# Gate logits of a Sinkhorn mixture of experts: float32 products from the accumulators in place of products on the split forms

## The chip, the cores and the metric

One core of one Trainium2 chip. The metric is the device time of one execution in microseconds, the median of several runs. Half a per cent of it is 10.6 us.

## The reference

Three parts run in a row. A linear attention on features gives x (2304 tokens by 512). A feed-forward with squared relu maps it: `h = relu(x @ w_in)`, `x = (h*h) @ w_out`. Then comes a mixture of 8 experts whose gates are made doubly normalised (a Sinkhorn iteration):

```python
logits = x @ w_gate
logits = logits - logits.max()
P = np.exp(logits)
for _ in range(8):
    P /= P.sum(1, keepdims=True) + 1e-09
    P /= P.sum(0, keepdims=True) + 1e-09
    P *= N / E
for e in range(E):
    out += P[:, e:e + 1] * (np.maximum(x @ w1[e], 0.0) @ w2[e])
```

The change concerns the line `logits = x @ w_gate` (2304x512 by 512x8) and the moment at which the Sinkhorn iteration starts.

## The kernel before

**Number forms.** TensorE (PE) runs almost everything on float32r operands. To keep precision, each operand is split into a high part (a cast on ScalarE, ACT) and a low part (a subtraction on VectorE, DVE); `split_form`, L604 to L606, makes both. A product is then three matmuls: high by high, high by low, low by high.

**First feed-forward.** Four passes of 512 hidden units. In the last pass (L749 to L779, `last`) the tokens are six blocks of 384. A block is four hidden tiles (`layer1`, then `split_square`) and the second layer (`layer2_square`), whose results DVE adds into the accumulators `accT` (L582). Side work is hung into this order by hand: a list `side` of generators, of which `tick()` (L558) advances the first by one step. There are six ticks a block: one after each hidden tile (L764), two inside the second layer (L583).

**Forms of x.** The second feed-forward works on pairs of blocks (768 tokens, three pairs) with seven products in place of eight, so it wants seven forms of x for each pair: four blocks of x and three further sums (t1 to t4 with the names of L627). `forms(q)` (L615) makes them for pairs 0 and 1 as side work in blocks 2 to 5 of the last pass, seven steps each, and writes them to DRAM (`xv`). The forms of pair 2 are made late, inside the second feed-forward, by `last_form` (L708, stores at L733).

**Gate logits.** They are computed from the split forms. `gate_weights` (L546) makes two padded stationary tiles `wg1`, `wg2` from w_gate. In `forms`, after a form that is one of the four in `USES` (L609), `wg1` meets its high part and `wg2` its low part (L645: 40 matmuls of 384 columns over both pairs). Then the 16 rows are turned into token order by four groups of three PE transposes (L657) and land in `lt`. For pair 2 the nested `logits` (L924) does it the other way round in the first layer of step 2: the form is the stationary operand, 16 columns of weights move, into spare columns of a PSUM bank (L935: 60 matmuls).

**Second feed-forward.** 16 passes (two for each expert) by three pairs give 48 steps, `order` (L673), numbered n = 0 to 47. First the first layer of step 0 runs alone (L1057 to L1063). Then, in the loop at L1069, "step n" is the second layer of n beside the first layer of n+1, seven slots each, with two ticks a slot. A slot of a layer is `product` (L862): 12 matmuls of 384 columns. `load_forms` (L695) keeps four forms of x loaded ahead on the SP queue.

**Sinkhorn.** `sinkhorn` (L809) is side work, added after step 1 (L1111), when `logits` has done pair 2. It adds the two halves of `lt` (L810), reduces a maximum, sends it through DRAM on the SP queue (store L813, load L815), waits eight ticks, and does eight rounds of three ticks. A round is nine small DVE instructions (L825 to L830, L837 to L840) around one float32 matmul of 8 columns (L835), which sums over partitions into spare columns of a first-layer bank. At its end four stores write the gates to DRAM (`prT`, L851).

**Use of the gates.** `load_gate` (L854) loads a gate on the SP queue. After step 3, `gate_first` (L1030) is added to the side work: it multiplies the accumulators of pair 0 by the gate of expert 0 (L1038), and so on for pairs 1 and 2. From step 5 on the hidden values of expert 1 and later are gated as they are made (L958).

**Order.** The Tile framework places the instructions of each engine in one fixed order, by the order in which they were traced and by what a planner takes to be ready. `issue_after` puts instructions behind a named one on its engine. Each engine then works in order.

Of the kernel before, what the change touches and what calls it, by code (L numbers as in the profile page):

```python
# [8 lines left out]
F32 = mybir.dt.float32  # L9
# [11 lines left out]
def tile_features_attention__moe__sinkhorn_moe(  # L21
# [19 lines left out]
    P = 128  # L41
# [496 lines left out]

    wg = mb.tile([P, KD, NE], F32, name="wg")
    nc.sync.dma_start(wg, w_gate.rearrange("(k p) e -> p k e", p=P))  # L540
    wg1 = mb.tile([P, KD, P], F32R, name="wg1")
    wg2 = mb.tile([P, KD, P], F32R, name="wg2")
    lt = mb.tile([P, NTT, 2 * NE], F32, name="lt")
    pr = mb.tile([P, NTT, NE], F32, name="pr")

    def gate_weights():  # L546
        z = hp.tile([P, 512], F32, tag="r", bufs=HB["r"], name="z")
        nc.gpsimd.memset(z, 0.0)
        z = z.rearrange("p (k m) -> p k m", k=KD)
        nc.vector.tensor_copy(wg1, z)  # L550
        nc.vector.tensor_copy(wg2, z)
        nc.vector.tensor_copy(wg1[:, :, 0:NE], wg)
        nc.vector.tensor_copy(wg2[:, :, 0:NE], wg)
        nc.vector.tensor_sub(wg1[:, :, NE : 2 * NE], wg, wg1[:, :, 0:NE].bitcast(F32))
# [53 lines left out]

    USES = {"b21": [(0, 1)], "t1": [(1, 0)], "b11": [(0, 0), (1, 0)], "b22": [(1, 1)]}  # L609

# [4 lines left out]
    def forms(q, pool):  # L615
# [8 lines left out]
        pg = [psm.tile([P, 512], F32, tag="sm", name="psg") for _ in range(2)]  # L624
        done = [0, 0]
        of = {}
        for nm in ("b21", "t1", "b11", "b22", "t2", "t4", "t3"):  # L627
# [14 lines left out]
            for blk, k in USES.get(nm, ()):  # L642
                for i in range(KH):
                    for w, part in ((wg1, 0), (wg2, 1)):
                        nc.tensor.matmul(  # L645
                            pg[blk][:, :NB], w[:, KH * k + i], v[:, part, i],
                            start=(done[blk] == 0), stop=(done[blk] == 4 * KH - 1 + 2 * KH * blk),
                        )
                        done[blk] += 1
            yield  # L650
        for blk in range(2):
            gs = pool.tile([2 * NE, NB], F32, tag="gs", name="gs")
            nc.scalar.copy(gs, pg[blk][: 2 * NE, :NB])
            pt = psm.tile([P, 4, 2 * NE], F32, tag="sm", name="pt")
            nt = NB // P
            for i in range(nt):
                nc.tensor.transpose(pt[:, i], gs[:, i * P : (i + 1) * P], ident[: 2 * NE, : 2 * NE])  # L657
            i0 = 2 * NB * q // P + blk * nt
            nc.scalar.copy(lt[:, i0 : i0 + nt], pt[:, :nt])
            yield  # L660
# [88 lines left out]
    for p in range(1, N1):  # L749
# [10 lines left out]
        for bi, (t0, n) in enumerate(blocks):  # L760
# [12 lines left out]
            if bi == 0 and p == 1:  # L773
                gate_weights()
# [376 lines left out]
```

## Time and profile before

| what | us |
|---|---|
| runs | 2109.52, 2110.79, 2118.28 |
| median | 2110.79 |
| the profiled execution | 2115.51 |
| its span, first to last instruction | 2113.7 |

1.8 us of the profiled execution lie outside its span, and it stands 4.7 us above the median. In views of the trace an engine's name stands before the line of the kernel; PE is the matmul itself and PEld the load of its stationary operand, which runs beside the matmul ahead of it. An arrow "a<-b" is output from inputs, and "[5.33 <-DVE hv L606]" says that the engine had been idle for 5.33 us and what ended it.

### The profile page before, as it was taken

Reading aid. Unit: us, or ns where it says so; the run is one execution under the profiler, and the core shown is the slowest. Engines: PE = TensorE matmul, PEld = TensorE weight load, DVE = VectorE, ACT = ScalarE, POOL = GpSimd, SP = SyncE. Lnnn points to the kernel's source line nnn. Section 1 sums busy time; section 2 is a strip of 40 time slices with the busy share of each in tenths; the row PEclk is TensorE's granted clock in tenths of the full one; section 3 lists DMA queues with packets and bytes.
Section 4 is the critical chain, followed back from the end, with each engine's and each line's share of the span. In section 5 each row is a group of like instructions: output and inputs, shape, how many; then the busy total and the mean of one; then the engine's idle time right before and its main releaser. Section 6 shows DMA issues by size and latency. Waiting matters only on the chain.

```text
span 2113.7 us, 31720 instructions
## 1 busy us (share of the span) xinstructions
PE 2066.9 (98%) x12376; PEld 1928.1 (91%) x12376; DVE 1731.3 (82%) x2168; ACT 873.7 (41%) x1505; POOL 765.6 (36%) x426
## 2 busy tenths in 40 slices
PE   8999999999999998899999999999999999999998
PEld 5556679888999998899999999999999999999998
DVE  4888665766567787799989889899898998989986
ACT  6786644222234552433433334333333333333332
POOL 3342300010105442534545435444344444444431
PEclk9999999999999999999999999999999999999999
DMA  4444232100136454767666776666766667676663
GB/s 112 109 106 120 72 115 71 60 29 32 55 148 243 183 195 136 235 226 251 220 226 204 237 246 227 224 211 225 252 221 224 226 222 242 224 227 235 209 203 120
DMA packets 184340, 376.47 MB, mean 178 GB/s; under 512 B 73600, under 2 KB 114560, under 8 KB 184192
## 3 DMA queue, kind: packets, MB, share of 16 engines
q1 hardware_dynamic: 184192, 374.44, 53.6%
q8 instruction: 99, 1.62, 0.3%
q14 instruction: 49, 0.40, 0.1%
HBM read 349.32 MB, written 24.93 MB: 177 GB/s over the span
## 4 chain that ended last, share of the span: by engine, by line
PE 83%; DVE 10%; DMA 4%; ACT 2%; issue 1%; SPq 0%; POOL 0%; DVEq 0%; ACTq 0%; POOLq 0%
PE psb L869 30%; PE psa L869 29%; PE ps L241 6%; PE ps L242 6%; PE ps L243 6%; DVE xl L606 2%; DMA rb<-rden 1%; DVE acc L1008 1%; PE kvp L350 1%; PE psn L406 1%; DVE hv L606 1%; PE zp L357 1%; DVE r L958 1%; DVE w2v L606 1%; PE psd L415 1%
## 5 line engine op out<-in xcount | busy, mean ns | idle before, releaser
L869 PE MATMUL psa<-xl,xh 128*128 128x384 f32 x2400 | 448.4, 336 | 7.2 <-DVE xl L606 4.2
L869 PE MATMUL psb<-xl,xh 128*128 128x384 f32 x2400 | 446.7, 335 | 4.4 <-DVE xl L606 1.7
L869 PEld LDWEIGHTS psa<-xl,xh 128*128 128x128 f32 x2400 | 420.4, 189 | 8.8 <-DVE xl L606 5.0
L869 PEld LDWEIGHTS psb<-xl,xh 128*128 128x128 f32 x2400 | 419.8, 188 | 5.9 <-DVE xl L606 2.3
L897 POOL TENSOR_TENSOR t<-r,r 128x768 f32<-128x768 f32 x96 | 208.7, 2174 | 492.3 <-DVE r L958 453.4
L897 POOL TENSOR_TENSOR t<-r,t 128x768 f32<-128x768 f32 x96 | 232.3, 2419 | 22.8 <-ACT r L962 12.2
L606 DVE TENSOR_TENSOR xl<-t,xl 128x768 fp32r<-128x768 f32 x128 | 187.0, 1463 | 1.4 <-ACT xl L605 1.2
L1008 DVE TENSOR_TENSOR acc<-psb,acc 128x768 f32<-128x768 f32 x163 | 155.0, 951 | 39.7 <-PE psb L869 36.3
L1008 DVE TENSOR_TENSOR acc<-psa,acc 128x768 f32<-128x768 f32 x161 | 153.0, 950 | 37.3 <-PE psa L869 34.0
L869 PE MATMUL psb<-xl,w2v 128*128 128x384 f32 x960 | 180.2, 334 | 0.0
L869 PE MATMUL psa<-xl,w2v 128*128 128x384 f32 x960 | 180.2, 334 | 0.0
L605 ACT CAST xl<-t 128x768 fp32r<-128x768 f32 x128 | 107.3, 838 | 154.8 <-POOL t L897 64.5
L869 PEld LDWEIGHTS psb<-xl,w2v 128*128 128x128 f32 x960 | 167.5, 188 | 0.0
L869 PEld LDWEIGHTS psa<-xl,w2v 128*128 128x128 f32 x960 | 167.4, 188 | 0.0
L605 ACT CAST xl<-r 128x768 fp32r<-128x768 f32 x96 | 80.4, 838 | 160.2 <-PE psa L869 77.2
L606 DVE TENSOR_TENSOR xl<-r,xl 128x768 fp32r<-128x768 f32 x96 | 134.7, 1403 | 7.1 <-ACT xl L605 7.1
L390 POOL PARTITION_ALL_REDUCE eq<-eq x64 | 88.8, 1429 | 141.5 <-ACT eq L389 141.5
L241 PE MATMUL ps<-xh,w0h 128*128 128x288 f32 (+3 forms) x384 | 130.8, 341 | 4.2 <-ACT r L262 3.4
L242 PE MATMUL ps<-xl,w0h 128*128 128x288 f32 (+3 forms) x384 | 129.5, 338 | 0.0
L243 PE MATMUL ps<-xh,w0l 128*128 128x288 f32 (+3 forms) x384 | 129.4, 338 | 0.0
L242 PE MATMUL ps<-gl,w1h 128*128 128x288 f32 (+3 forms) x384 | 127.1, 337 | 0.0
L243 PE MATMUL ps<-gh,w1l 128*128 128x288 f32 (+3 forms) x384 | 126.4, 337 | 0.0
(201 smaller groups left out, 3731.8 us busy)
## 6 DMA issues: line engine op xcount, KB each, us to landing
xl<-xv SPq DMA_DIRECT2D x329, 768.0 KB
wf<-in_moe_w_dram SPq DMA_DIRECT2D x32, 1024.0 KB
gate<-prT SPq DMA_DIRECT2D x45, 384.0 KB
xv<-xvs SPq DMA_DIRECT2D x14, 768.0 KB
raw<-in_moe_w_in_dram SPq DMA_DIRECT2D x16, 512.0 KB
raw<-in_moe_w_out_dram SPq DMA_DIRECT2D x16, 512.0 KB
xv<-xl SPq DMA_DIRECT2D x7, 768.0 KB
qnat<-in_q_dram SPq DMA_DIRECT2D x16, 288.0 KB
```

The source lines that it names most:

```text
L241: nc.tensor.matmul(ps, ah, bh, start=first, stop=False)
L242: nc.tensor.matmul(ps, ah, bl, start=False, stop=False)
L243: nc.tensor.matmul(ps, al, bh, start=False, stop=last)
L350: nc.tensor.matmul(kvp[h * D : (h + 1) * D, : 2 * NF], t[:r, i, h], e, start=(i == 0), stop=(i == MT))
L357: ins = nc.tensor.matmul(zp[q0 : q0 + 32, : 2 * NF], ones[:r, :32], e, start=(i < 2), stop=(i >= MT - 1))
L390: nc.gpsimd.partition_all_reduce(eq[:, 1], eq[:, 0], P, bass_isa.ReduceOp.absmax)
L406: nc.tensor.matmul(ps[h * D : (h + 1) * D, :HALF], kv[:, a, h * D : (h + 1) * D], eqs[2 * c + h][:, a], start=(a == 0), stop=(a == 1),)
L605: nc.scalar.copy(v[:, 0], src)
L606: nc.vector.tensor_sub(v[:, 1], src, v[:, 0].bitcast(F32))
L869: ins = nc.tensor.matmul(ps[:, x, :NB], w[:, wi, k, cs], b[:, bi, k], start=first and k + i == 0, stop=k == KH - 1 and i == 2, skip_group_ ...
L897: nc.gpsimd.tensor_tensor(t[nm], x, y, ALU.subtract)
L1008: latest["dve"] = nc.vector.tensor_add(o, ps, o).ins
```

## The change

The logits of a block are taken from the accumulators `accT` directly, as float32 matmuls (stationary: 128 by 128 of `accT`; moving: 8 columns of `wg`), 12 for a block of 384 tokens. They become side work after each block of the last pass. With all of them done before the second feed-forward, `sinkhorn` is added ahead of the first layer of step 0, which gets a tick a slot. The padded weights, `lt`, the products on the forms, the transposes and the late `logits` go.

```diff
--- before.py
+++ after.py
@@ -535,23 +535,9 @@
         split_w(1, 1)
     hp1.close()
 
-
     wg = mb.tile([P, KD, NE], F32, name="wg")
     nc.sync.dma_start(wg, w_gate.rearrange("(k p) e -> p k e", p=P))
-    wg1 = mb.tile([P, KD, P], F32R, name="wg1")
-    wg2 = mb.tile([P, KD, P], F32R, name="wg2")
-    lt = mb.tile([P, NTT, 2 * NE], F32, name="lt")
     pr = mb.tile([P, NTT, NE], F32, name="pr")
-
-    def gate_weights():
-        z = hp.tile([P, 512], F32, tag="r", bufs=HB["r"], name="z")
-        nc.gpsimd.memset(z, 0.0)
-        z = z.rearrange("p (k m) -> p k m", k=KD)
-        nc.vector.tensor_copy(wg1, z)
-        nc.vector.tensor_copy(wg2, z)
-        nc.vector.tensor_copy(wg1[:, :, 0:NE], wg)
-        nc.vector.tensor_copy(wg2[:, :, 0:NE], wg)
-        nc.vector.tensor_sub(wg1[:, :, NE : 2 * NE], wg, wg1[:, :, 0:NE].bitcast(F32))
 
     side = []
 
@@ -605,9 +591,6 @@
         nc.scalar.copy(v[:, 0], src)
         nc.vector.tensor_sub(v[:, 1], src, v[:, 0].bitcast(F32))
 
-
-    USES = {"b21": [(0, 1)], "t1": [(1, 0)], "b11": [(0, 0), (1, 0)], "b22": [(1, 1)]}
-
     def part_of(q, k, j):
         t0 = 2 * NB * q + (j - 1) * NB
         return accT[:, KH * (k - 1) : KH * k, t0 : t0 + NB]
@@ -621,8 +604,6 @@
         def temp(nm):
             return pool.tile([P, KH, NB], F32, tag="t", bufs=2, name=nm)
 
-        pg = [psm.tile([P, 512], F32, tag="sm", name="psg") for _ in range(2)]
-        done = [0, 0]
         of = {}
         for nm in ("b21", "t1", "b11", "b22", "t2", "t4", "t3"):
             if nm[0] == "b":
@@ -639,25 +620,23 @@
             v = pool.tile([P, 2, KH, NB], F32R, tag="v", bufs=3, name="xvs")
             split_form(src, v)
             nc.sync.dma_start(xv[q, FORMS.index(nm)], v.bitcast(F32).rearrange("p a k n -> p (a k n)"))
-            for blk, k in USES.get(nm, ()):
-                for i in range(KH):
-                    for w, part in ((wg1, 0), (wg2, 1)):
-                        nc.tensor.matmul(
-                            pg[blk][:, :NB], w[:, KH * k + i], v[:, part, i],
-                            start=(done[blk] == 0), stop=(done[blk] == 4 * KH - 1 + 2 * KH * blk),
-                        )
-                        done[blk] += 1
             yield
-        for blk in range(2):
-            gs = pool.tile([2 * NE, NB], F32, tag="gs", name="gs")
-            nc.scalar.copy(gs, pg[blk][: 2 * NE, :NB])
-            pt = psm.tile([P, 4, 2 * NE], F32, tag="sm", name="pt")
-            nt = NB // P
-            for i in range(nt):
-                nc.tensor.transpose(pt[:, i], gs[:, i * P : (i + 1) * P], ident[: 2 * NE, : 2 * NE])
-            i0 = 2 * NB * q // P + blk * nt
-            nc.scalar.copy(lt[:, i0 : i0 + nt], pt[:, :nt])
-            yield
+
+    def logits(t0):
+
+        nt = NB // P
+        ps = psm.tile([P, 512], F32, tag="sm", name="psg")[:, : nt * NE].rearrange("p (t e) -> p t e", e=NE)
+        first = None
+        for k in range(KD):
+            for t in range(nt):
+                with tc.issue_after(first) if first else ExitStack():
+                    ins = nc.tensor.matmul(
+                        ps[:, t], accT[:, k, t0 + t * P : t0 + (t + 1) * P], wg[:, k],
+                        start=first is None, stop=k == KD - 1, skip_group_check=t > 0,
+                    )
+                first = first or ins.ins
+        nc.scalar.copy(pr[:, t0 // P : t0 // P + nt], ps)
+        yield
 
 
     xhv = xh.rearrange("p k n -> p (k n)")
@@ -770,15 +749,17 @@
                 else:
                     split_w(p + 1, 0)
             layer2_square(p, g, t0, n)
-            if bi == 0 and p == 1:
-                gate_weights()
             if bi < len(blocks) - 1:
                 next(bg, None)
                 next(bg, None)
+            if last:
+                side.append(logits(t0))
             if last and bi % 2 and bi < len(blocks) - 1:
                 side.append(forms(bi // 2, xs))
         if not last:
             split_w(p + 1, 1)
+    while side:
+        tick()
     ffn1.close()
 
 
@@ -807,7 +788,6 @@
     latest = {}
 
     def sinkhorn():
-        nc.vector.tensor_add(pr, lt[:, :, 0:NE], lt[:, :, NE : 2 * NE])
         mx = mb.tile([P, 1], F32, name="mx")
         nc.vector.tensor_reduce(mx, pr, AX.XY, ALU.max)
         nc.sync.dma_start(mxd.rearrange("a p -> p a"), mx)
@@ -919,27 +899,6 @@
         form("t4", t["t4"])
         yield
 
-    done = [0, 0]
-
-    def logits(nm, x):
-
-        nt = NB // P
-        o = spare["tile"][:, 0, NB : NB + 2 * nt * 2 * NE].rearrange("p (t e) -> p t e", e=2 * NE)
-        with tc.issue_after(spare["first"]):
-            for blk, k in USES.get(nm, ()):
-                n8 = 4 * KH + 2 * KH * blk
-                for kk in range(KH):
-                    for w, part in ((wg1, 0), (wg2, 1)):
-                        done[blk] += 1
-                        for t in range(nt):
-                            nc.tensor.matmul(
-                                o[:, blk * nt + t], x[:, part, kk, t * P : (t + 1) * P], w[:, KH * k + kk, : 2 * NE],
-                                start=False, stop=done[blk] == n8, skip_group_check=True,
-                            )
-        if nm == "b21":
-            i0 = 2 * NB * (NPR - 1) // P
-            nc.scalar.copy(lt[:, i0 : i0 + 2 * nt], o)
-
     def layer1(n):
         p, q = order[n]
         e = (p - N1) // NJ
@@ -972,8 +931,6 @@
             ins = product(ps, w1v[i], x, nm in ("p1", "p5", "p2"))
             if i == 0:
                 spare.update(tile=a, first=ins)
-            if n == NPR - 1:
-                logits(FORMS[i], x)
             load_forms(NS * n + i + 1 + XB)
             if nm == "p1":
                 sn["a"] = snap(a, "ma")
@@ -1055,8 +1012,10 @@
 
     w2n = split_forms(N1, 1, w2v, sum_weights)
     l1 = layer1(0)
+    side.append(sinkhorn())
     for i in range(NS):
         next(l1)
+        tick()
         next(w2n)
     for x in (l1, w2n):
         for _ in x:
@@ -1108,8 +1067,6 @@
         for x in (l1, l2, w1n, w2n):
             for _ in x:
                 pass
-        if n + 1 == NPR - 1:
-            side.append(sinkhorn())
         made = nmade
         if order[n][0] == N1 + NJ - 1:
             side.append(gate_first(order[n][1]))
```

## Rows read from the trace of the kernel before

**Rows 1.** The page's busy line, whole span.

```profile
PE 2066.9 (98%) x12376; PEld 1928.1 (91%) x12376; DVE 1731.3 (82%) x2168; ACT 873.7 (41%) x1505; POOL 765.6 (36%) x426
```

**Rows 2.** Stretches: us, busy by engine, granted clock, DMA share, GB/s.

```profile
682.00:711.00 29.00, 29.00 (x168) 28.71 (x167) 22.73 (x18) 17.74 (x23) 14.53 (x7) 1.00 0.64 244
711.00:743.00 32.00, 32.00 (x198) 32.00 (x198) 23.31 (x21) 18.36 (x26) 14.44 (x8) 0.95 0.39 148
717.00:720.00 3.00, 3.00 (x11) 3.00 (x10) 3.00 (x3) 0.84 (x2) 1.97 (x1) 0.50 0.00 0
774.00:803.00 29.00, 27.22 (x158) 26.54 (x157) 25.96 (x45) 9.99 (x14) 8.38 (x4) 1.00 0.40 137
816.00:824.00 8.00, 6.07 (x23) 6.08 (x24) 7.90 (x9) 1.67 (x2) 3.56 (x2) 0.60 0.05 18
861.00:868.00 7.00, 6.26 (x23) 6.26 (x24) 4.76 (x6) 1.35 (x2) 0.00 (x0) 0.58 0.95 365
```

**Rows 3.** Waits of PE, 743 to 866 us: total, times, longest.

```profile
PE psb L869 <- DVE hv L606: 5.3, 1, 5.3
PE psa L869 <- DVE xl L606: 4.2, 2, 3.5
PE psa L869 <- ACT xl L605: 1.7, 1, 1.7
PE psb L869 <- ACT mu L884: 1.2, 1, 1.2
...
PE psb L869 <- DVE cr L837: 0.3, 1, 0.3
```

**Rows 4.** DVE in order of time, after the last round.

```profile
842.84 0.34 DVE L848 STREAM_TRANSPOSE tp<-pad 128x160 f32<-128x160 f32 x1
...
859.26 0.96 DVE L1038 TENSOR_TENSOR acc<-acc,gate 128x768 f32<-128x768 f32 x1 [7.62 <-DMA gate<-prT]
...
860.74 0.95 DVE L606 TENSOR_TENSOR hv<-r,hv 128x768 fp32r<-128x768 f32 x1
```

**Rows 5.** PE in order of time: products on the forms, last pass.

```profile
597.34 1.92 PE L645 MATMUL psg<-xvs,wg 128*128 128x384 f32 x10
599.10 0.34 PE L242 MATMUL ps<-gl,w1h 128*128 128x384 f32 x1
```

**Rows 6.** Groups by line, whole span: busy, mean ns, idle before and releaser.

```profile
L657 PEld LDWEIGHTS pt<-ident,gs 16*128 16x128 f32 x12 | 1.1, 135 | 1.2 <-issue 1.2
L835 PE MATMUL psb<-cs,ones 128*128 128x8 f32 x8 | 1.1, 213 | 0.0
```

**Rows 7.** PE in order of time: bursts of small products in step 1.

```profile
713.26 2.74 PE L935 MATMUL psa<-wg,xl 128*128 128x16 f32 x24
715.85 5.97 PE L869 MATMUL psb<-xl,xh 128*128 128x384 f32 x24
721.66 1.40 PE L935 MATMUL psa<-wg,xl 128*128 128x16 f32 x12
722.92 2.33 PE L869 MATMUL psa<-hv,xh 128*128 128x384 f32 x12
```

**Rows 8.** PE in order of time: one round's float32 product.

```profile
788.61 0.28 PE L835 MATMUL psb<-cs,ones 128*128 128x8 f32 x2
788.74 2.33 PE L869 MATMUL psa<-xl,w2v 128*128 128x384 f32 x12
790.91 2.24 PE L869 MATMUL psb<-xl,w2v 128*128 128x384 f32 x12
```

**Rows 9.** PE and DVE in order of time: the seam between the feed-forwards.

```profile
664.56 2.24 PE L869 MATMUL psa<-xl,xh 128*128 128x384 f32 x12
...
663.72 1.95 DVE L582 TENSOR_TENSOR acc<-ps,acc 128x384 f32<-128x384 f32 x4 [1.62 <-PE ps L243]
```

**Rows 10.** The SP queue in order of time: the maximum through DRAM.

```profile
745.47 0.32 SPq L813 DMA_DIRECT2D mxd<-mx  x1
752.09 0.32 SPq L815 DMA_DIRECT2D mr<-mxd  x1
752.50 0.38 SPq L703 DMA_DIRECT2D xl<-xv  x1
```

## The prediction

> **What bounds the kernel.** The busy line comes first: PE is busy 98% of the span, DVE 82%, the others under half [rows 1]. So time is gained by taking work off PE or by filling its holes. The table of stretches says where holes are: steps 0 and 1 (682 to 743 us) have none, step 3 (774 to 803) has 1.8 us, and it holds two places with a clock near 0.6 [rows 2]. The waits of PE from 743 to 866 us come to 15.2 us in eight lines, of which the rows show four and the last [rows 3]. They fall in the steps that hold the Sinkhorn rounds and the first use of a gate. DVE's own order tells the longest: the rounds end at 842.84, DVE then stands 7.62 us on the load of the gate (L1038), and behind it waits a low part (L606, 860.74) that PE wants [rows 4]. The kernel is thus bound by PE, and from step 3 to 866 us also by a Sinkhorn that ends too late.
>
> **The change, part by part.** The unit on PE is one matmul of 384 columns: ten from 597.34 to 599.10, 0.176 us each [rows 5]. For the second layers I take 0.174.
>
> *Off PE.* The 40 products on the forms (L645): 40 x 0.176 = 7.0 us. The twelve transposes: 1.1 us of loads and 1.2 us of idle before them, 2.3 [rows 6]; ACT's copies beside them go too, but ACT is at 41%. The 60 late products (L935): 24 of them from 713.26 to 715.85, so 0.108 each, and 12 from 721.66 to 722.92, 0.105 each [rows 7]: 60 x 0.107 = 6.4. After the burst of 24 the next 24 large matmuls take from 715.85 to 721.66, 5.81 us, where 24 x 0.174 = 4.18 is due; the granted clock there is 0.50, the lower of its two levels (1.2 GHz) [rows 2, 7]. That is 1.6 more. Sum: 17.3 us, all on the path, since PE has no hole in these places.
>
> *Off DVE.* The five casts of `gate_weights` and the addition L810 lie beside a full PE; nothing. Nor do I count the SP queue here: the products on forms issued no DMA.
>
> *On PE.* 72 float32 products (six blocks, three token tiles, four slices of 128). The trace has this shape, 128x128 stationary and 8 columns moving, in the rounds: eight rounds are recorded as 16 matmuls, eight in each of the two banks [rows 6], so one product is two records. One pair and the twelve large matmuls behind it take from 788.61 to 790.91, 2.30 us, and without the pair 12 x 0.174 = 2.09 [rows 8]: 0.21 for a product. The late burst gives the same, 2 x 0.108. 72 x 0.215 = 15.5 us. The Trainium skill (FP8 and Floating Point Precision, section TensorE Precision Notes) says that true float32 takes four passes through the array; by that, at one record a pass, I would estimate 31 us. The rows show two records and 0.21 us, so I keep that and leave four as a rival.
>
> *The clock.* A block's products are a burst of 24 records, as the one that was followed by the low clock; three bursts of 12 were not, of which one is shown [rows 7]. One case of 24 does not say that each does it, and large matmuls may come between the records. Bounds: none of six, 0; all six, 6 x 1.6 = 9.6. I take three, 4.8.
>
> *The seam.* The last block's products need its last additions, four in a row from 663.72 to 665.67, while PE goes on to the second feed-forward at 664.56 [rows 9]. If the products stand first in PE's order, it waits about 1.1 us; if the first large product is put ahead, not at all. I take 0.5, and 1.1 and 0 are the ends. In the other blocks a hidden tile (12 matmuls, 2.1 us) stands ahead and covers it. The six copies to `pr` are ACT's; PSUM has two buffers for them, so nothing waits.
>
> *Sinkhorn, moved.* It now starts at the first layer of step 0 (664), with its eight waiting ticks over by the beginning of step 0, and 25 more ticks at 14 a step end late in step 1, about 740 us, where they ended at 843. The gates are then in DRAM 100 us before they are wanted. So the wait of 5.3 us at 861 goes, and with it the low clock behind it: from 861 to 868 us PE is busy 6.26 us for 23 matmuls, and 23 x 0.174 = 4.0, so 2.3 more [rows 2, 3]. Gain 7.6. Next there is the low part itself, which DVE takes up 1.5 us after the gate [rows 4] and then at once; the multiplications (L1038, twelve of 0.96 us on DVE) spread over steps 4 to 6.
>
> The other seven lines of waits, 9.9 us, and the low clock of 816 to 824 (6.07 us for 23, 2.1 more) [rows 2, 3] belong to the rounds: PE and DVE hand each other small work in fixed orders, and forms stand behind it. They leave steps 2 to 4 and could come up in steps 0 and 1. DVE there is busy 22.7 of 29 and 23.3 of 32 us without rounds, against 26.0 of 29 in step 3 with them [rows 2]. So there is room for about 6 and 9 us, and four rounds of nine instructions of 0.15 to 0.6 us fit, just. On the other hand the late forms of pair 2 (L733, L606) pass there as well. Bounds: all 12.0 us vanish, or they double. I take the same price, no change.
>
> *Sinkhorn's DMAs.* The store of the maximum and its load (L813, L815) move on SP to the first layer of step 0, ahead of loads of forms (L703). The load waited on SP from 745.8 to 752.09, 6.3 us, and the next form was issued behind it [rows 10]. With four forms ahead at 2.1 us a slot, 8.3 us are covered, so I count nothing, and a rival below takes what lies past that. The four stores of the gates (L851) move from step 4 to step 1, between stores of pair 2; a slot there takes twice 2.1 us, and the same four forms cover them. On POOL it issues nothing.
>
> *Sum.* Off: 17.3 + 7.6 = 24.9. On: 15.5 + 4.8 + 0.5 = 20.8. Net 4.1 us less: the profiled 2115.5 becomes 2111.4. The profile stands 4.7 above the median, so the forecast for the median is 2110.8 - 4.1, about 2107.
>
> **The rivals.**
>
> *The rounds cost nothing in their new place.* For it: steps 0 and 1 have no hole on PE and more room on DVE than step 3, and the order of step 3 on was upset by a chain that also had to deliver the gates. Against: the rounds use the same banks and the same two engines. Then 12.0 us go as well: 2095.
>
> *SP starves the first layer.* It ends slower. The DMA share is 0.64 in step 0, against 0.40 in step 3 [rows 2], and the first layer of step 0 takes a form each 2.1 us with no second layer between. It decides from the point at which the hold, plus the landing of the next form (3.2 us, an estimate from the page's 768 KB for each form at the 244 GB/s of step 0), passes 8.3 us: a hold of 5.1. At the measured 6.3 it costs 1.2, which the forecast leaves out; at twice that, 12.6, it costs 7.5, and with a low clock of 2.3 behind it 9.8: 2107 + 10 = 2117.
>
> *Four passes.* The records show two, but a product of 8 columns could hide what one from `accT` does not. Then 15.5 more: 2123.
>
> *The change does not do what it says.* The order is the planner's: it may push the rounds back to where they were, since nothing wants them soon. Then the gate's wait stays, 7.6 back: 2115.
>
> **How the numbers follow.** Forecast 0.46, rounds free 0.25, SP 0.17, four passes 0.06, rounds pushed back 0.06. The forecast's own range is 2098 to 2116: three clock drops more or fewer (4.8) and a third more or less for the rounds (4.0). Half a per cent, 10.6 us, is about what a measurement of this kernel can tell from no change, so faster means under 2100.2 and slower over 2121.4. Faster: 0.19 of the rounds' 0.25 and 0.07 of the forecast, 0.26. Slower: 0.07 of SP's, 0.04 of the passes', 0.02 of the forecast with everything at its dear end, 0.13. The rest is 0.61. The range for 8 in 10 reaches from 2093 (rounds free, one drop fewer) to 2122 (SP, three drops more).
>
> **What the profile would show.** Right: no L645, L657, L935; 144 records of the new product, 0.108 us apart; the rounds from about 685 to 740 us; no wait on `gate<-prT`; holes of PE, if any, ahead of 745 us. Wrong: records spaced wider or four to a product; a form's load as the releaser of PE at 670 to 690; a hole at 860 as before; or the low clock behind each block's burst, which would take the gain away.

## The result and the profile after

The changed kernel takes 2135.71 us (median of six runs, 2125.35 to 2141.7) against 2111.62 us (six runs of the kernel before beside them, 2109.52 to 2118.28): 1.0106 times as long, 95% interval 1.0079 to 1.0134. That is slower by more than the half per cent that can be told from no change, and above the range of the prediction. The profiled execution took 2137.54 us, its span 2135.8.

The page's busy line answers to [rows 1]: PE is busy for 13 us more, and the span is 22 us longer.

```profile
PE 2080.0 (97%) x12408; PEld 1939.4 (91%) x12408; DVE 1745.6 (82%) x2162; ACT 873.3 (41%) x1502; POOL 767.8 (36%) x425
```

The stretches of [rows 2] again, with 743 to 774 us added (columns as there), and ahead of them the last pass of the first feed-forward:

```profile
552.97:675.35 122.38, 122.38 (x733) 121.57 (x732) 73.61 (x112) 41.69 (x78) 12.36 (x10) 0.97 0.37 142
682.00:711.00 29.00, 17.87 (x90) 16.65 (x88) 13.03 (x15) 9.60 (x14) 12.87 (x8) 0.82 0.69 255
...
743.00:774.00 31.00, 23.38 (x125) 22.65 (x125) 26.35 (x48) 10.70 (x15) 9.99 (x6) 0.89 0.37 138
...
861.00:868.00 7.00, 7.00 (x42) 7.00 (x42) 6.08 (x8) 3.79 (x5) 1.29 (x1) 1.00 0.61 185
```

The late stretch is full now, at full clock, so the old wait on the gate is gone. The holes stand earlier: PE is idle for 11 of the 29 us from 682, where it had none, and for 7.6 of the 31 us from 743. The waits of PE from 470 to 1000 us name what it waited for (they answer to [rows 3]; the line of the large products, L869 before, is L849 now, and `split_form`'s low part, L606, is L592):

```profile
PE psa L849 <- DMA xl<-xv: 10.0, 2, 9.5
PE psa L849 <- DVE hv L592: 6.6, 1, 6.6
...
PE psa L815 <- DVE cs L810: 1.4, 1, 1.4
```

The first is the load of a form in the first layer of step 0. The other two lie where the Sinkhorn rounds now are (L805 to L820, the product on PE at L815): from 703.7 to 783.5 us, where the prediction had about 685 to 740.

**Where the 22 us lie.** Cut the two spans at the first product of the second feed-forward [rows 9]. In the kernel before, the last pass takes 552.25 to 664.56, 112.3 us, and what follows 2113.7 - 664.56 = 1449.1. In the changed kernel the last pass takes 122.4 and what follows 2135.8 - 675.35 = 1460.5. So 10.1 us are lost ahead of the seam and 11.4 behind it, although 8.0 us of late products and low clock were taken off there (6.4 + 1.6 in the prediction's terms). The other 0.7 us lie ahead of the last pass.

**Ahead of the seam.** The new products in PE's order of time, two bursts of them with what follows each:

```profile
617.65 2.74 PE L633 MATMUL psg<-wg,acc 128*128 128x8 f32 x24
620.25 0.52 PE L241 MATMUL ps<-xh,w0h 128*128 128x384 f32 x1
620.57 0.52 PE L242 MATMUL ps<-xl,w0h 128*128 128x384 f32 x1
...
659.48 2.74 PE L633 MATMUL psg<-wg,acc 128*128 128x8 f32 x24
...
662.34 0.34 PE L242 MATMUL ps<-xl,w0h 128*128 128x384 f32 x1
662.52 0.34 PE L243 MATMUL ps<-xh,w0l 128*128 128x384 f32 x1
```

A block's 12 products are 24 records in 2.60 us (617.65 to 620.25), 0.108 each, as forecast. After the burst at 617.65 the large matmuls start 0.32 us apart, at the lower clock (granted 0.50 from 620.5 to 623.5 us, 1.2 GHz), and after the one at 659.48 soon 0.18 apart, at the full clock. In this execution the clock fell after two of the five bursts before the seam, and after the sixth, at the seam itself.

**Behind the seam.** The SP queue in order of time (L682 loads a form, L793 stores the maximum, L795 loads it back, L712 stores late forms, L213 loads weights), then the copy of the last block's logits on ACT, and DVE's instructions ahead of the maximum:

```profile
662.71 0.86 SPq L682 DMA_DIRECT2D xl<-xv  x2
666.66 0.38 SPq L213 DMA_DIRECT2D wf<-in_moe_w_dram  x1
679.36 0.32 SPq L793 DMA_DIRECT2D mxd<-mx  x1
688.49 0.32 SPq L795 DMA_DIRECT2D mr<-mxd  x1
688.86 0.90 SPq L682 DMA_DIRECT2D xl<-xv  x2
```

```profile
675.54 0.18 ACT L638 COPY pr<-psg 128x24 f32<-128x24 f32 x1 [0.76 <-PE psg L633]
```

```profile
673.27 3.62 DVE L592 TENSOR_TENSOR w2v<-wf,w2v 128x512 fp32r<-128x512 f32 x2
...
679.04 0.29 DVE L792 TENSOR_REDUCE mx<-pr 128x1 f32<-128x144 f32 x1
```

No form is issued from 663.6 to 688.86. SP reaches the store at 667 and stands 12.2 us on it. The greater part, 8.7 us, passes before `pr` is complete: the sixth burst ends only at 675.35, and ACT's copy of it at 675.72. For the next 3.3 us DVE is busy with splits of weights, which stand ahead of the maximum in its order. Then SP stands 8.8 us on the landing of those 4 bytes for each partition (the two waits as the view of SP's waits gives them). PE uses up the four forms it has and stops:

```profile
683.87 2.24 PE L849 MATMUL psb<-xl,xh 128*128 128x384 f32 x12
695.57 3.87 PE L849 MATMUL psa<-xl,xh 128*128 128x384 f32 x12 [9.45 <-DMA xl<-xv]
```

The twelve matmuls after the hole take 3.87 us where 2.24 is usual: the lower clock again. The order on SP makes the hold: the store and the load are put ahead of the first layer's remaining forms, where the trace of the kernel before has thirteen more loads of forms and the seven late stores ahead of them.

### The profile page after: what moved, and what is told of

It reads as the page before. It is cut to its first block, busy times and chain, and to the rows that moved or that the text cites. A ratio compares the mean times of both kernels' runs of the same rounds, so it can differ in the third digit from the quotient of the medians.

```text
span 2135.8 us, 31775 instructions
## 1 busy us (share of the span) xinstructions
PE 2080.0 (97%) x12408; PEld 1939.4 (91%) x12408; DVE 1745.6 (82%) x2162; ACT 873.3 (41%) x1502; POOL 767.8 (36%) x425
## 4 chain that ended last, share of the span: by engine, by line
PE 85%; DVE 9%; DMA 3%; ACT 1%; issue 1%; SPq 0%; POOL 0%; DVEq 0%; ACTq 0%
PE psa L849 30%; PE psb L849 30%; PE ps L241 6%; PE ps L242 6%; PE ps L243 6%; PE kvp L350 1%; DMA rb<-rden 1%; PE psn L406 1%; DVE xl L592 1%; PE zp L357 1%; DMA xl<-xv 1%; DVE acc L965 1%; DVE w2v L592 1%; PE psg L633 1%; PE psd L415 1%
## 5 line engine op out<-in xcount | busy, mean ns | idle before, releaser
L849 PE MATMUL psa<-xl,xh 128*128 128x384 f32 x2400 | 452.1, 338 | 17.3 <-DMA xl<-xv 10.0
L849 PE MATMUL psb<-xl,xh 128*128 128x384 f32 x2400 | 446.8, 336 | 4.4 <-DVE ma L924 2.5
L849 PEld LDWEIGHTS psa<-xl,xh 128*128 128x128 f32 x2400 | 423.8, 190 | 20.4 <-issue 10.9
L849 PEld LDWEIGHTS psb<-xl,xh 128*128 128x128 f32 x2400 | 420.8, 189 | 6.0 <-DVE ma L924 2.8
L592 DVE TENSOR_TENSOR xl<-t,xl 128x768 fp32r<-128x768 f32 x128 | 185.1, 1447 | 0.9 <-ACT xl L591 0.9
L849 PE MATMUL psb<-xl,w2v 128*128 128x384 f32 x960 | 180.7, 335 | 0.0
L849 PE MATMUL psa<-xl,w2v 128*128 128x384 f32 x960 | 179.8, 334 | 0.0
L849 PEld LDWEIGHTS psb<-xl,w2v 128*128 128x128 f32 x960 | 168.1, 188 | 0.0
L849 PEld LDWEIGHTS psa<-xl,w2v 128*128 128x128 f32 x960 | 167.5, 188 | 0.0
L592 DVE TENSOR_TENSOR xl<-r,xl 128x768 fp32r<-128x768 f32 x96 | 136.8, 1425 | 0.8 <-ACT xl L591 0.8
```

What stands on the lines that cost most here:

```text
L592: nc.vector.tensor_sub(v[:, 1], src, v[:, 0].bitcast(F32))
L849: ins = nc.tensor.matmul(ps[:, x, :NB], w[:, wi, k, cs], b[:, bi, k], start=first and k + i == 0, stop=k == KH - 1 and i == 2, skip_group_ ...
```

## The experiments

After the result there were three suspects for the 24 us: the hold on SP, the rounds in their new place, and the clock after the bursts; the rival was that the float32 products themselves cost more than forecast. Edits are against the changed kernel unless it is said otherwise; each set has its own runs of the kernel before beside it.

### The hold on SP: later starts, and no trip through DRAM

`e1_start_late` starts the Sinkhorn after step 1, where the kernel before has it:

```diff
     l1 = layer1(0)
-    side.append(sinkhorn())
     for i in range(NS):
         next(l1)
-        tick()
...
+        if n + 1 == 2:
+            side.append(sinkhorn())
         made = nmade
```

> The changed kernel with Sinkhorn started where it was before, after step 1, and no ticks in the first layer; the float32 products stay. Theory A (the loss is the early start: the SP queue held in the first layer, and the rounds in steps 0 and 1): the last pass stays about 10 us longer, the late products' 8 us are saved, the wait for the gate near 860 is back, so 2111 to 2116, within 5 us of the kernel before. Theory B (the float32 products themselves are the loss): about the changed kernel's 2135, over 2128.

Measured: 2126.46 us, ratio 1.008 (1.0056 to 1.0103), far from the expected 2111 to 2116. SP in order of time shows why:

```profile
672.66 0.32 SPq L793 DMA_DIRECT2D mxd<-mx  x1
681.78 0.32 SPq L795 DMA_DIRECT2D mr<-mxd  x1
```

The store did not move with its tick, and PE stands 9.5 us on a form as in the changed kernel. In SP's order it stands behind the same transfers as in the changed kernel, the load of weights the last of them. The planner, it seems, places the reduction and its DMAs by when `pr` is complete, not by when they were traced. So this run did not test the hold. The rounds themselves did move back, which leaves 9 us less than in the changed kernel and still 16 more than in the kernel before.

`e2_start_step0` starts it one step earlier, at the beginning of step 0:

```diff
-    side.append(sinkhorn())
     for i in range(NS):
         next(l1)
-        tick()
...
     NRP = 2 * NB // P
+    side.append(sinkhorn())
     for n in range(NN):
```

> The changed kernel with Sinkhorn started at step 0 instead of the first layer alone. A slot then takes 4.2 us and four forms cover 16.6 us. Theory A1 (the hold of SP in the first layer is most of the loss): the wait of 9.5 us on a form goes with the low clock behind it, about 12 to 14 us, so 2121 to 2124. Theory A2 (the rounds among the late forms are most of it): 2130 to 2136, as the rounds stay in steps 0 to 2.

Measured: 2131.0 us, ratio 1.009 (1.007 to 1.0111). A hold of the same size stood in the first layer (PE's longest wait on a form is 9.0 us), with the store at the same place in SP's order; the 2131 that was expected of the dear rounds came out with the hold still there, so it speaks for neither.

`e3_no_dram` takes the trip through DRAM out, by a reduction over partitions on POOL:

```diff
-        nc.sync.dma_start(mxd.rearrange("a p -> p a"), mx)
-        mr = hp.tile([P, 2, NB], F32, tag="gate", bufs=2, name="mr")[:, 0, :P]
-        nc.sync.dma_start(mr, mxd.to_broadcast([P, P]))
+        mr = mb.tile([P, 1], F32, name="mr")
+        nc.gpsimd.partition_all_reduce(mr, mx, P, bass_isa.ReduceOp.max)
```

> The changed kernel with the maximum over partitions made by one all-reduce on POOL in place of the two DMAs through DRAM; the start stays in the first layer. Theory A1 (the hold of SP): no PE wait on a form's load between 680 and 700 us, 10 us of idle and some 4 us of low clock go, 2120 to 2125. Theory A2 (the rounds): 2130 to 2136, with the waits of 740 to 790 us unchanged.

Measured: 2135.24 us, ratio 1.0117 (1.0098 to 1.0135): nothing won. POOL in order of time:

```profile
683.39 0.38 POOL L794 PARTITION_ALL_REDUCE mr<-mx  x1 [6.42 <-issue]
690.45 1.25 POOL L662 TENSOR_TENSOR s<-wf 128x512 f32<-128x512 f32 x1 [6.69 <-issue]
```

The reduction is recorded with 0.38 us, but POOL stands 6.42 us ahead of it and 6.69 behind it, for nothing that the profile shows. POOL's part in splitting the weights is late by that, ACT waits 14.6 us for it, and PE's longest wait from 640 us on is 12.7 us, on ACT, where it was 9.5 on a form. The hold moved from SP to POOL. None of the three runs says what it costs.

`e4_no_rounds` leaves the eight rounds out:

```diff
-        for it in range(8):
+        for it in range(0):
```

> The changed kernel without the eight rounds (leaves them out: the gates are only the exponentials); the two DMAs of the maximum stay in the first layer. Theory A1 (the hold): 2126 to 2132, since the hold stays and only a few us of the rounds go. Theory A2 (the rounds): their 12 us of waits between 740 and 790 us and the low clock behind them go, 2116 to 2121.

Measured: 2108.84 us (ten runs), ratio 0.9991 (0.9981 to 1.0). That is below both of the expected ranges. So in their new place the rounds cost 2135.71 - 2108.84 = 26.9 us by the medians; by the difference of the two ratios it is 24. SP's hold is still in this kernel (waits of 12.3 and 8.2 us on L793 and L795).

### The maximum held back

The later starts work once the reduction is tied to what DVE last did. `e5_max_held0` starts at step 0 (as e2) with

```diff
-        nc.vector.tensor_reduce(mx, pr, AX.XY, ALU.max)
+        with tc.issue_after(latest["dve"]):
+            nc.vector.tensor_reduce(mx, pr, AX.XY, ALU.max)
```

> Start at step 0, and the maximum (the DVE instruction that feeds the store) put behind the newest accumulation of DVE at that point, so that store and load follow the first layer's loads of forms in SP's order. The runs so far show that the tick alone does not set SP's order: with any start the store stood on SP from 660 us, behind only four loads of forms. Theory A (the hold of SP costs about 14 us, the rounds beside the late forms about 25 against 12 before): no wait of PE on a form near 685 us, 2118 to 2124. Rival (the hold is covered, as was written): no change against start at step 0 unheld, 2131.

Measured: 2120.99 us, ratio 1.0062 (1.0046 to 1.0078). The wait of 9.5 us on a form is gone; 3.8 and 1.7 us on forms are left.

`e6_max_held1` has the same hold-back and starts after step 0:

```diff
+        if n + 1 == 1:
+            side.append(sinkhorn())
```

> Start after step 0, the maximum held behind DVE's newest accumulation there. Theory A: no hold, and the gates ready before they are wanted; the rounds lie in steps 1 to 3, priced between 12 (old place) and 25 (steps 0 and 1): 2103 to 2116. Rival (the price of the rounds does not depend on their place): 12 to 14 us, 2102 to 2106.

Measured: 2120.59 us, ratio 1.0056 (1.0041 to 1.0071), above both expected ranges: the rounds did not get cheaper one step later.

`e7_max_held2` starts after step 1, so that only the place of the logits differs from the kernel before:

```diff
+        if n + 1 == 2:
+            side.append(sinkhorn())
```

> Start after step 1 as in the kernel before, the maximum held behind DVE's newest accumulation. This leaves of the change the float32 products alone. Theory A: 6 to 10 us more in the last pass, 8 us less for the late products, the rounds and the gate's wait as before: 2108 to 2113, the kernel before within 3 us. Rival (the products are slower than their 0.108 us a record, by the low clock behind them): 2116 or more.

Measured: 2117.69 us, ratio 1.0037 (1.0023 to 1.0051), in the range of the rival with low clock behind the products. Once the store no longer holds SP, no earlier start is seen to be better than the old one: 2120.99, 2120.59, 2117.69 from the earliest to the latest, with intervals that overlap.

`e8_max_held2_no_rounds` is e7 without the rounds (the `range(0)` of e4).

> As the last one, without the eight rounds (leaves them out: the gates are only the exponentials). Theory A: against the same without rounds but with SP held (2109) the hold's 14 us go: 2094 to 2098. Rival (the hold is no part of it): 2106 to 2110.

Measured: 2099.9 us, ratio 0.9957 (0.994 to 0.9973), between the two expected ranges. Without rounds, e4 and e8 differ by the hold and by the place of the little that is left of the Sinkhorn: 8.9 us by the medians, 7 by the ratios, and 10.9 by the profiles behind the seam (1435.3 and 1424.4). Of these 10.9, PE stands 7.2 us longer in e4, and the other 3.7 are the same work taking longer, as it does at the lower clock behind the hole. Against e8, whose set is the same, the rounds without the hold cost 21.1 us started at step 0 (e5), 20.7 after step 0 (e6) and 17.8 after step 1 (e7), there with the gate's wait in it. The longer waits on forms among PE's waits from 640 us on, first in e4, then in e8:

```profile
PE psa L849 <- DMA xl<-xv: 9.0, 2, 8.8
```

```profile
PE psa L850 <- DMA xl<-xv: 2.5, 2, 1.8
```

### Rounds in the old place, the hand-off, and the bursts

`e11_before_no_rounds` is the kernel before without its rounds:

```diff
-        for it in range(8):
+        for it in range(0):
```

> The kernel before without the eight rounds (leaves them out), for the price of the rounds and of the gate's wait in the old place, by itself. Theory A: the profile's 9.9 us of waits, 2.1 of low clock and 7.6 of the gate's wait go together, 19.6: 2110 becomes 2089 to 2092. Rival (part of these waits has another releaser that comes last next): 2095 to 2102.

Measured: 2092.62 us, ratio 0.9908 (0.9895 to 0.9921). In the old place the rounds and the gate's wait behind them cost 18.8 us (19 by the ratio); the prediction had 12.0 + 7.6 = 19.6 from the trace alone. In this kernel's trace the late burst of 24 is followed by the full clock (24 large matmuls from 713.15 to 717.40), so the 1.6 us of [rows 7] do not stand in it.

`e9_no_handoff` is the changed kernel with the rounds on DVE, but without the product on PE that sums over partitions:

```diff
-            ps = spare["tile"][:, 1, NB + it * NE : NB + (it + 1) * NE]
-            with tc.issue_after(spare["first"]), tc.issue_after(latest["pe"]):
-                nc.tensor.matmul(ps, ones, cs, start=False, stop=True, skip_group_check=True)
...
-            nc.vector.tensor_scalar(cr[:, 0], ps, 1e-9, None, ALU.add)
+            nc.vector.tensor_scalar(cr[:, 0], cs, 1e-9, None, ALU.add)
```

> The changed kernel with the rounds' product on PE left out (the sum over partitions is missing: each partition divides by its own column sum); all nine DVE instructions of a round stay. It tells what in the rounds costs 25 us between the changed kernel (2135) and the same without rounds (2109). Theory H (the hand-off: PE and DVE wait for each other through the product and its bank): most of it goes, 2109 to 2118. Theory L (the DVE instructions themselves, in DVE's fixed order ahead of the forms that PE waits for): most stays, 2124 to 2135.

Measured: 2115.69 us (ten runs), ratio 1.0022 (1.0013 to 1.0031). Without the products between DVE and PE 20.0 of the 26.9 us go (18 of 24 by the ratios); the eight products alone are 16 records of some 0.108 us, 1.7. The small DVE work that is left costs 6.9. Not all of the 20 is standing. Behind the seam the two profiled executions differ by 20.2 us (all that follows the first product, the changed kernel first, then e9; and e9 where the changed kernel has its hole, 743 to 774 us):

```profile
675.35:2135.80 1460.45, 1424.51 (x8153) 1417.45 (x8153) 1285.78 (x1292) 553.07 (x747) 646.50 (x319) 0.99 0.64 216
```

```profile
674.44:2114.70 1440.26, 1412.51 (x8138) 1406.36 (x8137) 1280.07 (x1292) 551.88 (x747) 645.28 (x319) 1.00 0.65 219
743.00:774.00 31.00, 29.11 (x166) 28.79 (x167) 30.31 (x48) 16.77 (x25) 13.89 (x8) 1.00 0.51 153
```

PE is idle for 8.2 us less in e9 (35.9 and 27.7) and busy for 12.0 less. The sixteen records are 1.7 of the 12.0; the other 10.3 is the same work done faster: the granted clock of the first 240 us is 0.93 in the changed kernel and 0.99 in e9. So the rounds cost holes and, in about the same amount, lower clock. That it stands behind the holes is seen at 695.57 above and at 747.23 below; it was not followed for every stretch of it. Of the waits from 640 us on, the one on `hv` falls from 6.6 to 2.5, while the hold on SP stays:

```profile
PE psa L846 <- DMA xl<-xv: 10.0, 3, 8.5
...
PE psa L846 <- DVE hv L592: 2.5, 1, 2.5
```

`e10_spread` is e7 with a block's 12 products in two halves, a tick apart:

```diff
                 first = first or ins.ins
+            if k == 1:
+                yield
```

> The kernel with the products alone (start after step 1, maximum held), each block's 12 products split into two ticks of six, so that four of the six bursts of 24 records become two of 12. Theory C (a burst of 24 is often followed by the low clock, 1.6 us each, three of six on average): one or two drops fewer in the last pass, so 2 to 3 us less than 2117.7: 2114 to 2116, the last pass 120 to 121 us long. Rival (the drops come from elsewhere): no change, 2117 to 2118, the last pass 122 to 125.

Measured: 2113.2 us (twelve runs), ratio 1.0012 (1.0004 to 1.0021), 4.5 us under e7. The stretch of its last pass:

```profile
550.77:670.03 119.26, 119.26 (x734) 118.46 (x732) 73.14 (x112) 41.56 (x78) 12.12 (x10) 1.00 0.38 146
```

The clock is full throughout, and the pass takes 119.3 us, where e7's took 123.8 with low clock in it after three bursts and one more at the seam. One trace would not show that the halves did it, since e1 has whole bursts and full clock. All traces together do: with whole bursts (the changed kernel, e1 to e9), the lower clock starts between 0.6 us before and 1.2 us after the end of 30 of the 60 bursts, and it starts nowhere else in these last passes. With halves (e10, e12 to e14) it follows one of the eight bursts that are still of 24 records, and none of the 40 shorter ones. So the bursts of 24 bring the lower clock, about every second time, and 119.3 - 112.3 = 7.0 us is what the products cost without it (the forms' products and transposes taken off).

### Can pacing save it?

Open then was whether the rounds are dear because their chain crowds steps 0 and 1. Both kernels have e10's halves and the held maximum. `e12_paced_step0` starts at step 0 and gives each round six ticks, with its two DVE groups tied to what DVE last did; `e13_paced_step1` starts after step 0 with four ticks a round:

```diff
-            nc.vector.tensor_reduce(rs, pr, AX.X, ALU.add)
+            with tc.issue_after(latest["dve"]):
+                nc.vector.tensor_reduce(rs, pr, AX.X, ALU.add)
...
-            yield
-            yield
+            for _ in range(3):
+                yield
...
-            nc.vector.tensor_scalar(cr[:, 0], ps, 1e-9, None, ALU.add)
+            with tc.issue_after(latest["dve"]):
+                nc.vector.tensor_scalar(cr[:, 0], ps, 1e-9, None, ALU.add)
...
-            yield
+            for _ in range(3):
+                yield
```

(shown for e12; e13 has `range(2)` in both places).

> Start at step 0, maximum held, bursts split as before, and the rounds spread out: six ticks a round in place of three, their DVE pieces behind the newest accumulation. Theory P (PE and DVE stand for each other since the rounds follow each other as fast as the planner lets them; with the time that the early logits give, PE need not wait): the rounds' 20 to 25 us fall to under 10 and no wait for the gate, 2100 to 2108, faster than the kernel before. Rival (each hand-off costs its 2 to 3 us whatever the pace): 2114 to 2120.

> The same from step 1, with four ticks a round. Theory P: 2100 to 2108. Rival: 2113 to 2118.

`e14_spread_step1` is e13 at the old pace of three ticks, without the two ties:

```diff
             if k == 1:
                 yield
...
+        if n + 1 == 1:
+            side.append(sinkhorn())
```

> Start after step 0, maximum held, bursts split, rounds at the old pace: the comparison for the paced ones. By the runs so far 2120.6 less some 4 us for the split bursts: 2115 to 2118, slower than the kernel before by 5 to 8 us.

Measured: e12 2114.02 us (1.0015, 0.9999 to 1.0031), e13 2112.79 (1.001, 0.9998 to 1.0022), e14 2118.56 (1.0047, 1.0031 to 1.0062). The pace and the two ties together are worth 5.8 us between e13 and e14, not the ten or more that was hoped for (2100 to 2108), and e12 lies where the rival had it. Less of it may be theirs: of the 7.8 us between the two profiled executions 3.5 lie ahead of the seam, where the two kernels do the same. What is left in e13 is again mostly a wait on a form, 6.5 us, and two on low parts, 4.5 together.

No version found here beats the kernel before; e10, e12 and e13 come to within 0.15% of it.

## Why the prediction was wrong

The prediction forecast a net gain of 4.1 us; the median came out 24.1 us later. The leave-out runs cut this into three terms, each the difference of two kernels that differ by it (first by the medians, in brackets by the ratios of their own sets, whose differences are multiplied by 2111):

| term | runs | measured, us | forecast, us |
|---|---|---|---|
| products and clock, without rounds and hold | e8 - e11 | +7.3 (10) | 15.5 + 4.8 + 0.5 - 17.3 = +3.5 |
| the hold on SP | e4 - e8 | +8.9 (7) | 0 |
| rounds and gate, new place less old | (after - e4) - (before - e11) | 26.9 - 18.8 = +8.1 (5) | 0 - 7.6 = -7.6 |

The intervals of the ratios, added in squares, leave the terms uncertain by some 4, 4 and 7 us. The profiles, cut at the seam, give 5.2 (10.1 ahead of it, -4.9 behind it), 10.9 and 5.3 (25.2 - 19.9). So the first term is not clearly off, and the errors of the second, 7 to 11 us, and of the third, 13 to 16, are clear of the noise. That the rounds with the gate's wait are dearer in the new place than in the old one is itself not clear; that they did not get 7.6 cheaper is.

**Off PE and on PE: right.** The three old products are gone, and the group of the new one answers to the forecast of 144 records:

```profile
L633 PE MATMUL psg<-wg,acc 128*128 128x8 f32 x144 | 16.6, 254 | 0.0
```

72 products at 0.216 are 15.5 us; less the 9.3 us of L645 and L657 that lay in the last pass, 6.2 were due, and e10 shows 7.0. The rival of four passes is out: with 31 us of products the last pass would have grown by 21.7. The Trainium skill (FP8 and Floating Point Precision, section TensorE Precision Notes) has four passes for true float32; each product here is two records, 0.216 us in all, and the measurement decides. The burst at 659.48 and the one at the seam, 672.60 to 675.35, start without idle time, so the 0.5 us for **the seam** was not needed either.

**The clock: right in size, in part by luck.** Three drops of 1.6 us were forecast, as the middle between none and six; no row spoke for three. The traces have from none (e1) to four (e5, e6, e7, e9) of six, 30 of 60 in all, and e7 against e10 takes 4.5 us. With three drops, the last pass was due at 112.3 + 6.2 + 4.8 = 123.3; it took 122.4 with two before the seam. Behind the seam 8.0 us should have come back, and e8 (1424.4) against e11 (1429.3) shows 4.9. The 1.6 us of low clock could not: e11's late burst was not followed by any, so that term too depends on the execution. PE is busy 6.7 us less in e8, about the 6.4 that were due, and stands 1.8 us longer, on forms.

**Wrong: "With four forms ahead at 2.1 us a slot, 8.3 us are covered, so I count nothing."** The cover was as described, and PE stopped when the four were used up. The hold was not 6.3 us but 22, for two reasons. The prediction took from [rows 10] only the load's wait on the store, and left out that the store itself waits for the maximum: 12.2 us here, for the last block's logits first and then for DVE's splits, against 2.3 in the kernel before, where DVE did the addition L810 and the reduction at once. And it placed the store by its tick, beside the running first layer, while the planner placed it ahead of that layer's loads; e1 shows that the tick does not decide this. The rival "SP starves the first layer" had the mechanism, and asked from which length of hold it decides; only the length it was given, 6.3 or twice that, was too short. By its rule 22 us would cost 16.9 (22 + 3.2 - 8.3); PE stood 9.5, since the first 8.3 us of the hold passed ahead of 675.35, before the first form was used.

**Wrong: "Bounds: all 12.0 us vanish, or they double. I take the same price, no change."** By the leave-out runs the rounds cost 24 to 27 us in the new place, and 21 where no hold stands beside them (e5 less e8): at or near the dear bound of 24, not 12.0. The gate's wait did go, with the 7.6 us of the prediction (e11 bears the sum of 19.6 out, though not its two parts one by one), but it was paid back within the rounds. The reason given was room on DVE, 6 and 9 us of idle time in steps 0 and 1. Room is not what the rounds need: e9 shows that three quarters of their price goes with the product on PE, by which each round is handed from DVE to PE and back. In the profiles that part is 8.2 us of holes, 10.3 of lower clock and 1.7 of the products themselves. How a hole comes about, the longest shows (PE, then DVE, in order of time):

```profile
740.25 0.34 PE L849 MATMUL psa<-hv,xh 128*128 128x384 f32 x1
747.23 3.50 PE L849 MATMUL psa<-hv,xh 128*128 128x384 f32 x11 [6.64 <-DVE hv L592]
```

```profile
735.91 1.25 DVE L819 TENSOR_SCALAR cr<-cr 128x8 f32<-128x8 f32 x1
737.07 0.95 DVE L592 TENSOR_TENSOR xl<-latex,xl 128x768 fp32r<-128x768 f32 x1
737.94 1.96 DVE L820 TENSOR_TENSOR pr<-pr,cr 128x144 f32<-128x144 f32 x1
739.82 2.32 DVE L592 TENSOR_TENSOR xh<-wf,xh 128x512 fp32r<-128x512 f32 x1
...
742.27 2.35 DVE L592 TENSOR_TENSOR xl<-latey,xl 128x768 fp32r<-128x768 f32 x1
744.54 1.77 DVE L806 TENSOR_SCALAR rs<-rs 128x18 f32<-128x18 f32 x1
746.22 0.95 DVE L592 TENSOR_TENSOR hv<-t,hv 128x768 fp32r<-128x768 f32 x1
```

PE waits for the low part of `hv`. ACT has made its high part by 738.89 (738.05 + 0.84), but DVE comes to the low part only at 746.22, after the instructions of a round and three splits, the splits of pair 2's late forms (`latex`, `latey`) among them. These are the forms of which the prediction said in passing that they "pass there as well"; that was the place to take the dear bound. The eleven matmuls behind the hole take 3.50 us, where eleven take 2.2 at the full clock. The order is not the only suspect: four of the DVE instructions between 737.94 and 746.31 take 8.4 us (1.96, 2.32, 2.35, 1.77), where instructions of the same lines and shapes take 2.1 elsewhere (0.31, 0.69, 0.95, 0.18), and the difference, 6.3, is nearly the whole hole. Whether these long instructions (see the last section) or the order makes the rounds dear here was not tried separately; that cause stays open.

**The gates in time, but for nothing.** Their stores were issued from 785.7 us on, not at about 740. No multiplication waited for them (the first is at 866 us), so a start as early as that had little to win: only the old 7.6 us, and e7's late start, in which DVE still waits 5.2 us for the gate, is no slower than the two earlier ones with the maximum held back.

**The other rivals.** The rounds were not free. They were not pushed back to their old place: the planner moved the maximum forward, not the rounds back.

## What to carry to other kernels

A DMA that is moved up a queue brings two waits with it, its own for its input and that of its reader for its landing, and the planner may place it earlier than the code reads; before counting it as covered, read in the new place when its producer can be done, not how long it waited in the old one. A chain that goes back and forth between two engines costs what each neighbour in the two fixed orders makes it wait, so its price has to be measured by leaving it out, in the old place and in the new one; idle time on the engines does not bound it, and the lower clock that goes with the holes can cost as much as they do (10.3 us beside 8.2 here). A burst of short matmuls can leave the lower clock to the work behind it, here after 30 of 60 bursts of 24 records, and cutting it into halves between large matmuls is a cheap trial.

## What was not expected of the hardware

**DVE beside POOL.** In the hole above three short DVE instructions take 1.25, 1.96 and 1.77 us that take 0.17, 0.31 and 0.18 elsewhere in the same rounds, and each ends within 0.2 us of a POOL instruction: at 737.16, 739.90 and 746.31, where POOL's end at 737.14, 739.73 and 746.28 (POOL in order of time):

```profile
734.57 2.57 POOL L877 TENSOR_TENSOR t<-r,r 128x768 f32<-128x768 f32 x1
737.21 2.52 POOL L877 TENSOR_TENSOR t<-r,t 128x768 f32<-128x768 f32 x1
...
743.77 2.51 POOL L877 TENSOR_TENSOR t<-r,t 128x768 f32<-128x768 f32 x1
```

The groups of the rounds' lines on DVE show what that comes to, first for the changed kernel (690 to 790 us), then for the kernel before (740 to 850 us):

```profile
L820 DVE TENSOR_TENSOR pr<-pr,cr 128x144 f32<-128x144 f32 x8 | 6.2, 773 | 0.2
L808 DVE TENSOR_TENSOR pr<-pr,rs 128x144 f32<-128x144 f32 x8 | 4.1, 512 | 0.2
L806 DVE TENSOR_SCALAR rs<-rs 128x18 f32<-128x18 f32 x8 | 4.1, 511 | 0.2
L810 DVE TENSOR_REDUCE cs<-pr 128x8 f32<-128x144 f32 x8 | 3.4, 424 | 0.1
L819 DVE TENSOR_SCALAR cr<-cr 128x8 f32<-128x8 f32 x8 | 2.4, 304 | 0.2
```

```profile
L840 DVE TENSOR_TENSOR pr<-pr,cr 128x144 f32<-128x144 f32 x8 | 5.1, 631 | 0.2
L830 DVE TENSOR_REDUCE cs<-pr 128x8 f32<-128x144 f32 x8 | 3.5, 432 | 0.2
L826 DVE TENSOR_SCALAR rs<-rs 128x18 f32<-128x18 f32 x8 | 3.0, 376 | 0.1
L828 DVE TENSOR_TENSOR pr<-pr,rs 128x144 f32<-128x144 f32 x8 | 2.4, 305 | 0.2
...
L839 DVE TENSOR_SCALAR cr<-cr 128x8 f32<-128x8 f32 x8 | 1.4, 170 | 0.2
```

Of these lines the four that are not reductions take 16.8 us against 11.9, the reduction 3.4 against 3.5. The Trainium skill (SBUF — State Buffer, section Who interferes with whom) says that DVE and GpSimd share one pair of ports, taken for a whole instruction by whichever comes first: DVE copies and `tensor_scalar` can want it, as can instructions with two inputs in SBUF, and a reduction never does. These rows agree with that; what these 4.9 us are worth in the kernel's time, no run here shows.

**A store of 512 bytes.** The load behind the store of the maximum, 4 bytes a partition, waited 6.3 us for its landing in the kernel before [rows 10] and 8.8 in the changed one.

**The all-reduce on POOL.** Around a recorded 0.38 us POOL stands some 13 us (e3), for nothing that the profile shows; why stays open.

**The clock is not the same from run to run.** Six bursts with the same records were followed by anything from no low clock to four stretches of it, though in the changed kernel's last pass, for one, PE has no gap. Single executions of that kernel spread over 16 us, from 2125.35 us at a mean granted clock of 0.992 to 2141.7 at 0.986.
